# One of the last weight tiles of a decode step, shared out unevenly over the DMA engines

## The chip, the cores and the metric

The kernel runs on one core of a Trainium2 chip. The metric is the device time of one execution in microseconds (us). Everything is in float32.

## What is computed

One token goes through a layer norm and then through two parallel branches, sliding-window attention over a cache and a gated MLP; both are added to the token.

```
xn = layernorm(x)                                   # x: 1 x 1 x 1024
q  = xn @ wq                                        # 1024 x 4096, 32 heads of 128
k, v = the last 4096 positions of the cache         # 4 key/value heads, 8 query heads each
attn = softmax(q k^T / sqrt(128)) v @ wo            # wo: 4096 x 1024
mlp  = (gelu_tanh(xn @ w_gate) * (xn @ w_up)) @ w_down   # 1024 x 3584, 1024 x 3584, 3584 x 1024
y  = x + attn + mlp
```

With one token, every weight and cache row is used once: 94 MB are read.

## The kernel before, in words

All large tensors pass through one buffer in SBUF, `ring` (128 partitions, 176 KB each). `pieces` lists 20 pieces in the order in which they are loaded, each with its place in the ring and its size: wq in two pieces, keys, gate, values and up in two each, wo in two, and w_down in eight. `pump()` records the loads of all pieces whose place is free of pieces still in use; `done()` frees a piece when its last reader is recorded, and pumps again. All these loads are issued by SyncE (SP), in that order, on one DMA queue; three small loads of x go by ScalarE's queue. A load spans all 128 partitions.

w_down has 3584 rows; partition p holds 28 consecutive rows, and "tile t" is row t of every partition, a block of 128 partitions x 1024 columns (4 KB per partition, 512 KB in all). The pieces of w_down are tiles 0 to 11, 12 to 19, 20 and 21, 22 and 23, and then 24, 25, 26 and 27 alone; tile 27 comes in two halves of columns. So the loads get smaller toward the end.

TensorE and VectorE share the contractions. A tile on VectorE is one multiply-add into `part` (L213); a tile on TensorE is four or eight matmuls by `mm` (L158). The end of the program is written out by hand: tile 24 on TensorE into `sums`, then the product of `unit` with VectorE's partial sum `out_part` (a view of `part`), tile 25, an addition into `x_out` on VectorE, tile 26, and for each half of tile 27 its matmuls, one addition and two stores (one issued by SP, one by ScalarE).

The program is recorded first. `Program.add` notes what each operation reads and writes and derives what it must wait for; each DMA is a lane of its own with a semaphore of its own, and a reader waits until that semaphore has reached 16. `plan` drops waits that are already covered, `emit` writes the instructions.

Of the kernel before, what the change touches and what calls it, by code (L numbers as in the profile page):

```python
# [10 lines left out]
P = 128  # L11
# [13 lines left out]

RING = 176 * KB
SCRATCH = 1024
HEADS_A = [0, 2, 4, 6, 8, 10, 12, 14]
HEADS_B = [0, 2, 4, 6, 8, 10, 12, 14]
HID_A = [0, 2, 4, 6, 8]  # L30
# [5 lines left out]
class Program:  # L36

    def __init__(self, nc):  # L40
        self.nc = nc
        self.ops = []
        self.seen = {}
        self.engines = dict(pe=nc.tensor, dve=nc.vector, act=nc.scalar, pool=nc.gpsimd, sp=nc.sync)

    @staticmethod
# [5 lines left out]
        hi = lo + 1 + sum(abs(s) * (n - 1) for s, n in ap.ap[1:])  # L52
        return ap.tensor.name, p0, p0 + count, lo, hi

    def add(self, engine, emit, reads, writes, dma=False, tag=None):
        op = dict(engine=engine, emit=emit, dma=dma, needs={}, tag=tag, id=len(self.ops),
                  boxes=[self.box(a) for a in writes + reads])
        op["lane"] = f"dma{op['id']}" if dma else engine
        for writing, aps in ((False, reads), (True, writes)):
            for ap in aps:  # L60
                name, p0, p1, lo, hi = self.box(ap)
                for wrote, q0, q1, a, b, other in self.seen.get(name, ()):
                    if not (writing or wrote) or q0 >= p1 or p0 >= q1 or a >= hi or lo >= b:
                        continue
                    if other["lane"] == op["lane"] and (engine == "pe" or not wrote):
                        continue
                    lane = other["lane"]
                    op["needs"][lane] = max(op["needs"].get(lane, -1), other["id"])
        for writing, aps in ((False, reads), (True, writes)):
            for ap in aps:  # L70
                name, p0, p1, lo, hi = self.box(ap)
                kept = self.seen.setdefault(name, [])
                if writing:
                    kept[:] = [
                        k for k in kept
                        if not (p0 <= k[1] and k[2] <= p1 and lo <= k[3] and k[4] <= hi)
                    ]
                kept.append((writing, p0, p1, lo, hi, op))
        self.ops.append(op)
        return op  # L80

    def plan(self):
        known = {e: {} for e in self.engines}
        for op in self.ops:
            mine = known[op["engine"]]
            waits = []
            for lane, other in sorted(op["needs"].items(), key=lambda n: -n[1]):
                if mine.get(lane, -1) >= other:
                    continue
                waits.append(other)  # L90
                for k, v in self.ops[other]["after"].items():
                    mine[k] = max(mine.get(k, -1), v)
            op["waits"] = waits
            op["after"] = dict(mine)
            op["after"][op["lane"]] = op["id"]
        for op in self.ops:
            for other in op["waits"]:
                self.ops[other]["told"] = True
        counts = {}
        for op in self.ops:  # L100
            if op["dma"]:
                op["rank"] = 16
            elif op.get("told"):
                counts[op["engine"]] = counts.get(op["engine"], 0) + 1
                op["rank"] = counts[op["engine"]]
# [41 lines left out]
def decode_layer(nc, x, k_cache, v_cache, wq, wo, w_gate, w_up, w_down, out):  # L147
# [29 lines left out]
    def dve(call, reads, writes, engine="dve"):  # L177
        prog.add(engine, call, reads, writes)
# [9 lines left out]
    def add(o, a, b):  # L188
        dve(lambda e: e.tensor_add(o, a, b), [a, b], [o])  # L189
# [24 lines left out]
            [i, factor, other], [o],  # L214
        )

    def dma(engine, o, i, reads=(), writes=(), tag=None):
        return prog.add(
            engine, lambda e: e.dma_start(o, i), list(reads), list(writes), dma=True, tag=tag  # L219
        )  # L220

    ring = sbuf("ring", P, RING)
# [2 lines left out]
    def rows(w, a):  # L225
        return w[512 * a:512 * (a + 1), :].rearrange("(p r) n -> p (r n)", r=4)

    def heads_of(a):
        return wo[2048 * a:2048 * (a + 1), :].rearrange("(p t) n -> p (t n)", p=P)

    hidden_rows = w_down.rearrange("(p t) n -> p t n", p=P)
# [12 lines left out]
    def load(kind, i, at, size):  # L244
        slot = ring[:, at * KB:(at + size) * KB]
        held[kind, i] = slot
        if kind == "v":
            src = v_cache[0, 2 * i:2 * i + 2, SK - WIN:, :].rearrange("g (p j) d -> p g (j d)", p=P)
            dma("sp", slot.rearrange("p (g n) -> p g n", g=2), src, writes=[slot], tag=(kind, i))
        elif kind == "k":  # L250
            src = k_cache[0, 2 * i:2 * i + 2, SK - WIN:, :].rearrange("g (s j) d -> s g (j d)", g=2, j=64)
            dma("sp", slot, src, writes=[slot], tag=(kind, i))
        elif kind == "d":
            lo, hi = i
            halves = 2 if lo == TD - 1 else 1
            wide = slot.rearrange("p (t n) -> p t n", n=D)
            for half in range(halves):
                cols = slice(half * D // halves, (half + 1) * D // halves)
                dst = wide[:, :, cols]
                dma("sp", dst, hidden_rows[:, lo:hi, cols], writes=[dst], tag=(kind, i, half))  # L260
        else:
            src = {
                "q": lambda: rows(wq, i), "g": lambda: rows(w_gate, i), "u": lambda: rows(w_up, i),
                "o": lambda: heads_of(i),
            }[kind]()
            dma("sp", slot, src, writes=[slot], tag=(kind, i))
# [4 lines left out]
    def pump():  # L271
        while queue:
            kind, i, at, size = queue[0]
            if any(at < hi and lo < at + size for lo, hi in live.values()):
                return
            load(*queue.pop(0))
            live[kind, i] = (at, at + size)
# [170 lines left out]
    p = rows_sb[:, 0, :]  # L448
# [159 lines left out]
    def head(t):  # L608
        return oz[:, 32 * t:32 * t + 64]
# [38 lines left out]
    def contract(kind, i, z, dve_tiles, rows):  # L648
        w = held[kind, i].rearrange("p (t n) -> p t n", n=D)
        count = w.shape[1]  # L650
        rest = [(z(t), w[:, t, :]) for t in range(count) if t not in dve_tiles]
        if rows:
            tiles_on_rows(rest)
        else:
            for pair in rest:
                tile_on_pe(*pair)
        for t in dve_tiles:
            tile_on_dve(z(t), w[:, t, :])
        done(kind, i)
# [38 lines left out]

    state["total"] = 2 * TO + 12 - len(HEADS_A + HEADS_B + HID_A)
    contract("o", 0, head, HEADS_A, True)  # L700
    contract("o", 1, lambda t: head(TO + t), HEADS_B, True)
    contract("d", (0, 12), column, HID_A, True)
    add(out_part, acc[:].rearrange("p a n -> p (a n)"), out_part)
    contract("d", (12, 20), lambda t: column(12 + t), HID_B, False)
    contract("d", (20, 22), lambda t: column(20 + t), HID_C, False)
    contract("d", (22, 24), lambda t: column(22 + t), HID_D, False)
    tile_on_pe(column(24), held["d", (24, 25)])
    tile_on_pe(unit[:], out_part)
    tile_on_pe(column(25), held["d", (25, 26)], True)
    add(x_out[:].rearrange("p f n -> p (f n)"), sums[:], x_out[:].rearrange("p f n -> p (f n)"))  # L710
    for half in range(2):
        half_on_pe(column(26), held["d", (26, 27)], half, True, False)
    stores = out.rearrange("a b (f c n) -> (a b) f c n", f=2, c=4)
    for half in range(2):
        half_on_pe(column(27), held["d", (27, 28)], half, False, True)
        add(y[:, half, :], acc[:, half, :P], x_out[:, half, :])
        for k, engine in enumerate(("sp", "act")):
            src = y[31 + 64 * k:33 + 64 * k, half, :]
            dma(
                engine, stores[0, half, 2 * k:2 * k + 2, :], src, reads=[src],  # L720
                tag=("out", half, k),
            )
# [25 lines left out]
```

## Time and profile before

| | us |
|---|---|
| median of 3 runs | 226.66 |
| lowest and highest | 226.65, 226.82 |
| profiled execution | 226.83 |
| its span in the profile | 225.5 |

| engine | share of the span busy |
|---|---|
| VectorE (DVE) | 64% |
| TensorE (PE) | 39% |
| ScalarE (ACT) | 12% |
| the 16 DMA engines, SP's queue (q1) | 97.5% |

A row of the profile names the line of the kernel, the engine, the operation, and what is written from what (`ring<-in_B_w_down` is a load of w_down into the ring, `SPq` the queue of SP that issues it). "us to landing" is the time from a load's issue until its data is there. DMA is the mean busy share of the 16 DMA engines. A wait stands in brackets behind a row, with what ended it.

### The profile page before, as it was taken

How to read it: one execution, taken by the hardware profiler on the slowest of the kernel's cores; microseconds unless marked ns; L12 is line 12 of the kernel's file. 1: busy time of each engine (PE TensorE's matmuls, PEld its weight loads, DVE VectorE, ACT ScalarE, POOL GpSimd, SP SyncE). 2: the span in 40 equal slices, each digit the busy share in tenths (PEclk: the TensorE clock that was granted, in tenths of full speed). 3: DMA queues.
4: the chain of work that ended last, by engine and by line, in shares of the span. 5: the costliest groups of instructions: out<-in, count | busy, mean ns of one | idle time of the engine just before them, and what ended most of it. 6: DMA issues, size and time to landing. Idle time of an engine off the chain costs nothing.

```text
span 225.5 us, 1396 instructions
## 1 busy us (share of the span) xinstructions
PE 87.5 (39%) x574; PEld 34.8 (15%) x574; DVE 143.2 (64%) x127; ACT 26.3 (12%) x45; POOL 0.7 (0%) x6
## 2 busy tenths in 40 slices
PE   1200000007699007989002537137339204408475
PEld 0100000006263002462000111011002001002131
DVE  7500998499727990000998699869538804938691
ACT  2000000004555001482000300200000000000000
POOL 1000000000000000000000000000000000000000
PEclk9999999999999755999755667857855855965889
DMA  9899899899989999999999998999999999999992
GB/s 373 372 395 535 372 395 535 349 405 478 468 349 426 465 401 503 427 397 471 427 397 392 433 509 387 478 391 491 419 395 488 419 395 413 427 439 442 382 405 111
DMA packets 3317, 94.46 MB, mean 419 GB/s; under 512 B 350, under 2 KB 366, under 8 KB 1008
## 3 DMA queue, kind: packets, MB, share of 16 engines
q1 hardware_dynamic: 3288, 94.38, 97.5%
q8 instruction: 4, 0.07, 0.1%
q10 hardware_dynamic: 24, 0.01, 0.0%
q14 instruction: 1, 0.01, 0.0%
HBM read 94.38 MB, written 0.00 MB: 419 GB/s over the span
## 4 chain that ended last, share of the span: by engine, by line
DMA 65%; DVE 26%; PE 7%; issue 1%; SPq 1%; DVEq 0%
DVE part L213 24%; DMA ring<-in_B_w_down 19%; DMA ring<-in_A_wq 18%; DMA ring<-in_B_w_gate 15%; DMA ring<-in_A_wo 13%; PE acc L158 3%; PE tp L163 2%; PE s_p L158 2%; DVE part L209 1%; SPq L219 1%; DVE rows_sb L186 0%; DVE part L189 0%; DVEq L118 0%; SPq L118 0%
## 5 line engine op out<-in xcount | busy, mean ns | idle before, releaser
L213 DVE SCALAR_TENSOR_TENSOR part<-ring,xz,part 128x3584 f32<-128x3584 f32 (+1 forms) x19 | 78.8, 4148 | 26.6 <-DMA ring<-in_B_w_gate 22.6
L163 PE MATMUL tp<-ident,ring 128*128 128x128 f32 x128 | 20.3, 303 | 44.4 <-DMA ring<-in_A_k_cache 42.8
L213 DVE SCALAR_TENSOR_TENSOR part<-ring,oz,part 128x1024 f32<-128x1024 f32 x15 | 19.3, 1285 | 9.9 <-DMA ring<-in_A_wo 9.4
L172 ACT ACTIVATE ring<-tp 128x512 f32<-128x512 f32 x32 | 18.1, 596 | 58.4 <-PE tp L163 58.0
L163 PEld LDWEIGHTS tp<-ident,ring 128*128 128x128 f32 x128 | 15.0, 152 | 51.2 <-DMA ring<-in_A_k_cache 42.9
L209 DVE TENSOR_SCALAR part<-ring,xz 128x3584 f32<-128x3584 f32 (+1 forms) x3 | 6.5, 2176 | 19.7 <-DMA ring<-in_A_wq 12.1
L158 PE MATMUL acc<-ring,oz 128*32 128x512 f32 x64 | 11.7, 899 | 16.8 <-DMA ring<-in_A_wo 16.8
L213 DVE SCALAR_TENSOR_TENSOR part<-ring,hz,part 128x1024 f32<-128x1024 f32 x10 | 12.8, 1285 | 6.1 <-DMA ring<-in_B_w_down 5.8
L158 PE MATMUL acc<-part,unit 128*32 128x448 f32 (+1 forms) x48 | 7.3, 742 | 22.3 <-DVE part L213 22.3
L158 PE MATMUL o_p<-ring,pT 128*32 128x512 f32 x64 | 11.0, 847 | 7.1 <-DMA ring<-in_A_v_cache 6.5
L158 PE MATMUL acc<-ring,hz 128*32 128x128 f32 (+1 forms) x60 | 8.0, 616 | 10.1 <-DMA ring<-in_B_w_down 10.1
L158 PE MATMUL s_p<-ring,qz 128*32 128x512 f32 x64 | 9.3, 598 | 0.0
L163 PE MATMUL tp<-ident,rows_sb 128*128 128x128 f32 x16 | 3.5, 361 | 12.0 <-ACT rows_sb L172 11.8
L158 PE MATMUL sums<-ring,hz 128*32 128x256 f32 x72 | 6.2, 482 | 4.7 <-DMA ring<-in_B_w_down 4.7
L158 PEld LDWEIGHTS acc<-ring,oz 128*32 128x32 f32 x64 | 2.5, 155 | 26.6 <-DMA ring<-in_A_wo 19.4
L158 PEld LDWEIGHTS acc<-part,unit 128*32 128x32 f32 x48 | 1.4, 126 | 26.4 <-DVE part L213 24.2
L172 ACT ACTIVATE rows_sb<-s_p,negm 128x512 f32<-128x512 f32 x2 | 1.4, 687 | 30.4 <-DVE negm L209 30.4
L158 PEld LDWEIGHTS o_p<-ring,pT 128*32 128x32 f32 x64 | 2.6, 149 | 14.5 <-issue 13.4
L158 PE MATMUL acc<-ring,xz 128*32 128x448 f32 x32 | 4.8, 767 | 0.0
L158 PEld LDWEIGHTS acc<-ring,hz 128*32 128x32 f32 x60 | 2.2, 135 | 15.8 <-issue 14.0
L163 PEld LDWEIGHTS tp<-ident,rows_sb 128*128 128x128 f32 x16 | 2.3, 179 | 15.5 <-ACT rows_sb L172 13.6
L158 PEld LDWEIGHTS sums<-ring,hz 128*32 128x32 f32 x72 | 2.4, 136 | 9.2 <-DMA ring<-in_B_w_down 7.3
(85 smaller groups left out, 47.8 us busy)
## 6 DMA issues: line engine op xcount, KB each, us to landing
ring<-in_B_w_gate SPq DMA_DIRECT2D x2, 7168.0 KB, 31.9
ring<-in_B_w_up SPq DMA_DIRECT2D x2, 7168.0 KB, 33.9
ring<-in_A_k_cache SPq DMA_DIRECT2D x2, 4096.0 KB, 39.7
ring<-in_A_v_cache SPq DMA_DIRECT2D x2, 4096.0 KB, 34.8
ring<-in_B_w_down SPq DMA_DIRECT2D x1, 6144.0 KB, 42.9
ring<-in_B_w_down SPq DMA_DIRECT2D x1, 4096.0 KB, 38.8
ring<-in_B_w_down SPq DMA_DIRECT2D x2, 1024.0 KB, 40.4
ring<-in_B_w_down SPq DMA_DIRECT2D x3, 512.0 KB, 42.0
```

Of the source, the lines that this page charges most:

```text
L158: "pe", lambda e: e.matmul(o, lhsT, rhs, start=start, stop=stop),
L163: prog.add("pe", lambda e: e.transpose(o, i, eye), [i, eye], [o])
L172: "act", lambda e: e.activation(o, i, func, scale=scale, **kw),
L209: dve(lambda e: e.tensor_scalar(o, i, s1, s2, op0=op0, **kw), reads, [o])
L213: lambda e: e.scalar_tensor_tensor(o, i, factor, other, op0=ALU.mult, op1=ALU.add),
L219: engine, lambda e: e.dma_start(o, i), list(reads), list(writes), dma=True, tag=tag
```

## The change

Tile 24 of w_down no longer comes as one transfer of 128 partitions but as ten. Each takes every second, fourth or eighth partition of some stretch, and together they take each of the 128 once: 64, 26, 13, 5, 5, 4, 2, 3, 3 and 3 partitions. All ten share one semaphore, and the reader waits until it has reached 160. All other pieces stay as they are.

```diff
+UNEVEN = 24
+SHARES = [
+    (0, 128, 2), (1, 102, 4), (3, 100, 8), (7, 40, 8), (47, 80, 8), (87, 112, 8), (119, 128, 8),
+    (105, 114, 4), (117, 126, 4), (107, 124, 8),
+]
...
-    def add(self, engine, emit, reads, writes, dma=False, tag=None):
+    def add(self, engine, emit, reads, writes, dma=False, tag=None, group=None):
...
-        op["lane"] = f"dma{op['id']}" if dma else engine
+        op["lane"] = engine
+        if dma:
+            first = self.groups.setdefault(group, op["id"]) if group else op["id"]
+            op["lane"] = f"dma{first}"
+            self.sizes[op["lane"]] = self.sizes.get(op["lane"], 0) + 16
...
-                    if other["lane"] == op["lane"] and (engine == "pe" or not wrote):
+                    if other["lane"] == op["lane"] and (engine == "pe" or dma or not wrote):
...
-                op["rank"] = 16
+                op["rank"] = self.sizes[op["lane"]]
...
             lo, hi = i
+            if lo == UNEVEN:
...
+                for share in SHARES:
+                    some = slice(*share)
+                    dma(
+                        "sp", slot[some, :], hidden_rows[some, lo, :], writes=[slot],
+                        tag=(kind, i), group=(kind, i),
+                    )
+                return
```

A triple in `SHARES` is first partition, end and step. On SP the loads of the pieces of w_down stand before the change in this order (partitions x elements of a partition; the three of 128x1024 are tiles 24, 25 and 26, the two of 128x512 the halves of tile 27):

```order
L219 DMA ring<-in_A_wo 128x16384 x2
L219 DMA ring<-in_B_w_down 128x12288
L219 DMA ring<-in_B_w_down 128x8192
L219 DMA ring<-in_B_w_down 128x2048 x2
L219 DMA ring<-in_B_w_down 128x1024 x3
L219 DMA ring<-in_B_w_down 128x512 x2
L219 DMA out_y<-part 2x128 x2
```

The first of the three is what the change replaces; the same stretch of SP after it (the same helper stands at L230 now):

```order
L230 DMA ring<-in_B_w_down 128x2048 x2
L230 DMA ring<-in_B_w_down 64x1024
L230 DMA ring<-in_B_w_down 26x1024
L230 DMA ring<-in_B_w_down 13x1024
L230 DMA ring<-in_B_w_down 5x1024 x2
L230 DMA ring<-in_B_w_down 4x1024
L230 DMA ring<-in_B_w_down 2x1024
L230 DMA ring<-in_B_w_down 3x1024 x3
L230 DMA ring<-in_B_w_down 128x1024 x2
L230 DMA ring<-in_B_w_down 128x512 x2
L230 DMA out_y<-part 2x128 x2
```

Nine issues more stand ahead of tiles 25, 26 and 27; the instructions of the other engines are the same in the same order.

More of the change, by code (lines that the diff above doesn't have):

```diff
@@ L43, in __init__ @@
         self.seen = {}
+        self.groups, self.sizes = {}, {}
         self.engines = dict(pe=nc.tensor, dve=nc.vector, act=nc.scalar, pool=nc.gpsimd, sp=nc.sync)
@@ L215, in multiply_add, with dma @@
         )
-    def dma(engine, o, i, reads=(), writes=(), tag=None):
+    def dma(engine, o, i, reads=(), writes=(), tag=None, group=None):
         return prog.add(
-            engine, lambda e: e.dma_start(o, i), list(reads), list(writes), dma=True, tag=tag
+            engine, lambda e: e.dma_start(o, i), list(reads), list(writes), dma=True, tag=tag,
+            group=group,
         )
@@ L254, in load @@
             lo, hi = i
+            if lo == UNEVEN:
+                assert sorted(p for s in SHARES for p in range(*s)) == list(range(P))
+                for share in SHARES:
[5 more added lines that the diff above has]
+                return
             halves = 2 if lo == TD - 1 else 1
```

## The prediction

> **What bounds the kernel now.** I read the page's DMA part first, then the end of the chain of waits, then the transfers and TensorE in the last microseconds.
>
> ```profile
> span 225.5 us, 1396 instructions
> DMA packets 3317, 94.46 MB, mean 419 GB/s; under 512 B 350, under 2 KB 366, under 8 KB 1008
> q1 hardware_dynamic: 3288, 94.38, 97.5%
> q8 instruction: 4, 0.07, 0.1%
> ```
>
> The 16 DMA engines are busy 97.5% of the span with the loads that SP issues: the kernel is a stream of weights. The question is only when the last byte of that stream arrives. The chain of waits ends so (start, length, what):
>
> ```profile
> 180.03 0.43 SPq L219
> 180.46 0.04 issue
> 180.50 42.73 DMA ring<-in_B_w_down
> ...
> 223.28 0.47 PE acc L158 x8
> 223.75 0.02 issue
> 223.77 0.29 DVE part L189
> ```
>
> The last half of tile 27 is the end of the chain; behind it stand four matmuls with their weight loads (0.47 us), one addition (0.29 us) and the stores, which the change leaves alone. So a last byte that comes x earlier ends the kernel x earlier, unless TensorE becomes late (below). How the stream ends is seen in the transfers from 220 to 224 us, in slices of 0.1 us (first row: busy tenths of the 16 engines; second: GB/s):
>
> ```profile
> DMA  9799998995645433322322112100000000000000
> GB/s 389 266 512 389 369 389 307 451 348 184 225 164 225 164 143 143 123 102 102 143 102 82 61 41 82 41 21 20 0 0 0 0 0 0 0 0 0 0 0 0
> ```
>
> This is the important row. To 220.9 us nearly all engines work; then the rate falls, and the last byte comes at 222.8. One engine carries 434/16 = 27.1 GB/s when all run (the mean GB/s of the stretch 45 to 100 us):
>
> ```profile
> 45.00:100.00 55.00, 31.73 (x204) 17.34 (x204) 31.34 (x19) 18.76 (x33) 0.00 (x0) 0.88 1.01 434
> ```
>
> So 143 GB/s at 221.5 is about five engines, 102 at 222.0 about four, some 60 (mean of the next three) two, and 20 at 222.7 one. I read the finishing times as 222.8, 222.65, 222.3 and 222.2 for the four latest, about 221.9 for a fifth, and 220.9 to 221.5 for the other eleven. They all move the same bytes, so five fell behind earlier. From 220.9 on the row sums to 2168 GB/s x 0.1 us = 217 KB; at 434 GB/s that is 0.50 us, so a perfect division would end at 221.4: no division of the rows can gain more than 1.4 us.
>
> One cause shows in the instruction queue (q8, page above: four packets, 0.07 MB, so 16 KB each). In the stretch 215 to 226 us:
>
> ```profile
> q8 instruction: 1, 0.02, 0.6%
> ```
>
> 0.6% of 16 engines x 11 us is 1.06 us of one engine for one fetch of 16 KB, which the engine's own rows wait out. Four fetches, each on one engine, would make four engines late by a microsecond or more, about what the tail shows. The rows do not name the engines. Following single packets through the trace, which no view prints, I find the four fetches on four different engines, and the two engines that carry the two-partition loads of x among the early ones.
>
> **The change, part by part.** Tile 24 is 128 rows of 4 KB, today eight on each engine. Ten transfers take its place. I take equal shares on the largest number of engines up to 16 that divides the partitions, counted from engine 0; the title's thirteen engines for 26 and 13 fit that. The 350 packets under 512 B bear out the division in a small case: 21 loads of 128 partitions leave 21 x 16 = 336 completion writes, and seven transfers of two partitions (three loads of x, four stores) leave 14 if each runs on two engines; 336 + 14 = 350. Then 64 rows give four to every engine, 26 and 13 give three more to engines 0 to 12, and 5, 5, 4, 2, 3, 3, 3 go to the lowest. Rows of tile 24: engines 0 and 1 fourteen, 2 thirteen, 3 ten, 4 nine, 5 to 12 seven, 13 to 15 four. [...]
>
> The price of a row comes from TensorE, which waits for each of the last tiles:
>
> ```profile
> start us, us, engine line op out<-in xcount [idle before <-releaser]
> 219.49 0.64 PE L158 MATMUL sums<-ring,hz 128*32 128x256 f32 x8 [0.62 <-DMA ring<-in_B_w_down]
> 219.94 0.62 PE L158 MATMUL sums<-part,unit 128*32 128x256 f32 x8
> 220.78 0.64 PE L158 MATMUL sums<-ring,hz 128*32 128x256 f32 x8 [0.21 <-DMA ring<-in_B_w_down]
> 222.03 1.04 PE L158 MATMUL acc<-ring,hz 128*32 128x128 f32 x24 [0.61 <-DMA ring<-in_B_w_down]
> 223.28 0.43 PE L158 MATMUL acc<-ring,hz 128*32 128x128 f32 x8 [0.21 <-DMA ring<-in_B_w_down]
> ```
>
> Tiles 24, 25 and 26 start at 219.49, 220.78 and 222.03: 1.27 us for eight rows, 0.157 us a row. So 13 to 15 finish 4 x 0.157 = 0.63 us earlier, 5 to 12 0.16 earlier, 4 is 0.16 later, 3 0.31, 2 0.79, 0 and 1 0.94.
>
> Which of them are late decides the sum. If the two latest and one of the next two are 13 to 15, their ends become 222.2, 222.0 and 221.7; the fourth, among 5 to 12, goes from 222.3 to 222.15; engines 0 to 2, if early (up to 221.2), come to 222.0 to 222.15. All meet near 222.2: 0.6 us less. If the latest stands among 5 to 12, 0.16 less; if it is 0 or 1, 0.94 more. Between these ends I take 0.6: the two engines that can be told, 0 and 1, are early and have 1.3 us of room for 0.94, and of the fourteen others, among which the four latest must be, nothing in the rows speaks against 13 to 15.
>
> Nine more completion writes on the lowest engines are bounded by 0 and by what the stream leaves idle: 2.5% (q1 at 97.5%) of the 1.27 us of a tile, 0.03 us for nine packets. I take 0.03.
>
> SP's issues:
>
> ```profile
> L219 SPq DMA_DIRECT2D ring<-in_B_w_down x9: 328/328/10887, 160.6 to 180.5; - x9
> 180.50 10.89 SPq L219 DMA_DIRECT2D ring<-in_B_w_down  x1
> ring<-in_B_w_down SPq DMA_DIRECT2D x3, 512.0 KB, 42.0
> 189.05 10.53 DVE L213 SCALAR_TENSOR_TENSOR part<-ring,oz,part 128x1024 f32<-128x1024 f32 x8 [9.43 <-DMA ring<-in_A_wo]
> 203.59 6.57 DVE L213 SCALAR_TENSOR_TENSOR part<-ring,hz,part 128x1024 f32<-128x1024 f32 x5 [4.00 <-DMA ring<-in_B_w_down]
> 213.30 6.57 DVE L213 SCALAR_TENSOR_TENSOR part<-ring,hz,part 128x1024 f32<-128x1024 f32 x5 [1.82 <-DMA ring<-in_B_w_down]
> ```
>
> Nine more at 0.33 us are 3.0 us of SP (3.9 at 0.43, the dearest unblocked step in the chain). Tiles 25, 26 and 27 are queued behind them. The cover is the distance from issue to landing, 42.0 us for tiles 24 to 26, so I cost them at nothing. One row warns: the very last issue took 10.89 us, to 191.4. Something was full. If it is full by packets per engine, engines 0 and 1 get fifteen more (six rows, nine completions). The tiles ahead pass nine packets of an engine each (eight rows and a completion), in 203.59 - 189.05 = 14.5 us and 213.30 - 203.59 = 9.7 us, so fifteen take 14.5 + 6/9 x 9.7 = 21 us: the last issue would go at about 212, still 8 us before its rows are due. The first share carries the slot's old wait, the others none, and no other engine waits for SP before the stores.
>
> What is late next: tile 24 at 218.9 and tile 25 at 220.2 find TensorE held by the product with out_part, which waits for VectorE:
>
> ```profile
> 219.92 0.16 PEld L158 LDWEIGHTS sums<-part,unit 128*32 128x32 f32 x8 [0.28 <-DVE part L213]
> ```
>
> It ends at 219.94 + 0.62 = 220.56, tile 25 at 221.2, and tile 26 comes at 221.4: TensorE stays ahead by 0.2 us, so all of the gain arrives.
>
> Sum: 226.83 (this profiled execution: span 225.5 and 1.33 around it) - 0.60 + 0.03 = 226.26. The median of the runs is 226.66, 0.17 lower; from it the forecast is **226.1**.
>
> **Rivals.** *Ports instead of engines (nothing, or a loss).* Perhaps the 27.1 GB/s belongs to the place written rather than to the engine. Then a late engine's partitions still have to take the same bytes, and handing its rows to others relieves nothing: while it writes its earlier rows, up to eight rows of tile 24 come into its partitions from elsewhere (up to 8 x 0.157 = 1.26 us), for which it saves eight rows and spends four (0.63) on foreign ones. Net between 0.2 less, where foreign rows fall into gaps, and 0.63 more; 226.5 to 227.3, middle 226.8. [...]
>
> *A late engine among 2 to 4 (slower).* If one of the four that end at 222.2 to 222.8 is engine 2, it ends 0.79 later, as engine 3 or 4 0.31 or 0.16: the kernel takes up to 0.79 us more, 226.7 to 227.45. It decides once engine 2 ends after 222.0 today (222.8 - 0.79). Against it: three of fourteen engines, and four late ones to place; for it: nothing names them.
>
> *The late ones are not 13 to 15, or the shares fall otherwise.* The latest among 5 to 12 gives 226.5; shares that spread over all 16 engines give 226.7. Two completion packets for two partitions speak against the latter.
>
> *The queue is full by transfers, not packets (slower).* If the 10.89 us came from nine transfers outstanding, the ten of tile 24 fill it alone: tile 25 could be issued only when the first shares have landed, near 218.5, and the engines run empty. The last store
>
> ```profile
> L219 SPq DMA_DIRECT2D out_y<-part x2: 257/294/331, 223.5 to 224.1; - x2
> ```
>
> is issued at 224.1 and the span ends at 225.5, so a transfer on empty engines takes over 1 us; one to three such gaps give 227.7 to 229.7. Against it: the oldest of the nine, the second half of wo, had landed by 189.05 (it releases VectorE there), and the issue went on only at 191.4, when packets of the next tile had passed.
>
> **How the numbers follow.** Relief of 13 to 15 as summed: 0.40, own range 225.9 to 226.2. Ports: 0.33, of which 0.25 within 0.2% and 0.08 slower. Not 13 to 15, or spread otherwise: 0.10, the same. Engine 2, 3 or 4 late: 0.10. Full queue: 0.07. A measurement of this kernel can tell about 0.2% (0.45 us) from no change. Faster 0.40; same 0.25 + 0.10 = 0.35; slower 0.08 + 0.10 + 0.07 = 0.25. Low is 225.9, the first case with 0.2 us to spare; high is 227.3, the end of the ports case, which leaves out the queue and a late engine 2.
>
> **What would show it.** In the slices from 220 us the fall should start later and be steeper, with the last byte near 222.2; the matmuls of tile 27's second half near 222.7. Packets under 512 B should be 350 - 16 + 16 + 13 + 13 + 5 + 5 + 4 + 2 + 3 + 3 + 3 = 401. If ports set the pace, the slices before 220.9 show lower rates than before and the last byte stays at 222.8 or later. A late low engine shows as one engine (20 to 27 GB/s) alone for up to a microsecond. A full queue shows as zeros in the slices. Wrong would be my numbering of engines or the guess that fetches hit the high ones.

## The result, and the profile after

The changed kernel takes 227.38 us (median of 8 runs, 227.13 to 227.74) against 226.75 for the kernel before (8 runs, 226.53 to 226.90): ratio 1.0028, 95% interval 1.0017 to 1.0039. It is 0.63 us slower, and outside the range that was given. The profiled execution is the slowest of the eight, 227.74 us. Its page:

```profile
span 226.4 us, 1405 instructions
DMA packets 3368, 94.46 MB, mean 417 GB/s; under 512 B 401, under 2 KB 417, under 8 KB 1059
q1 hardware_dynamic: 3339, 94.38, 97.6%
```

The bytes are the same, the engines are as busy as before (97.6% against 97.5%), and the 401 small packets are what the division of the shares called for. What changed is the rate. The transfers from 220 to 224 us after the change, in slices of 0.1 us (busy tenths of the 16 engines, GB/s), to be laid beside the row that the prediction started from:

```profile
DMA  9959999989899999866464456453432101000000
GB/s 369 492 225 430 410 369 451 430 348 451 328 410 430 348 389 471 307 225 225 184 246 184 184 205 246 164 205 123 184 123 82 41 21 41 0 0 0 0 0 0
```

The fall starts later, as forecast (221.6 instead of 220.9), but it isn't steeper: 184 to 246 GB/s is seven to nine engines at 27.1, and the last byte comes at 223.4 instead of 222.8. Half of the engines are late now, where five were: of the sixteen landings of the last transfer, eight come by 222.45 us and eight from 223.19 on; before, eleven came by 221.98 and five from 222.35 on. They fell behind earlier. From 214 to 224 us in slices of 0.25 us, first the kernel before:

```profile
DMA  9998979899998999999999999997543321000000
GB/s 393 459 459 360 492 328 426 361 410 426 393 475 328 410 426 360 426 377 410 442 377 434 361 426 377 393 410 262 213 156 123 123 90 57 33 0 0 0 0 0
```

and the kernel after:

```profile
DMA  9999798997999999999998999999999555431000
GB/s 459 426 393 492 328 459 361 377 475 311 492 328 279 279 311 229 262 262 262 262 295 262 344 344 377 393 410 410 369 393 369 197 197 229 180 139 57 16 0 0
```

The two agree to 217.0 us. Then the rate after drops to 229 to 311 GB/s, comes back to 344 at 219.5 and to 410 at 220.5; in these three microseconds tile 24 comes (its single landings, read from the trace, run from 216.9 to 220.3). All the while the first row shows 9: no engine is idle, each packet only takes longer. Single packets, which no view prints, say the same: those of 4 KB that start between 217.0 and 219.5 us take 0.23 to 0.25 us (medians of half microseconds, nine in ten over 0.21) where they took 0.16 before. As one stretch (DMA share and GB/s are the last two columns), before and after:

```profile
217.00:220.00 3.00, 1.67 (x32) 0.43 (x28) 2.80 (x3) 0.00 (x0) 0.00 (x0) 1.00 1.00 398
```

```profile
217.00:220.00 3.00, 1.29 (x16) 0.16 (x8) 2.54 (x3) 0.00 (x0) 0.00 (x0) 0.88 1.02 283
```

398 - 283 = 115 GB/s over 3 us are 345 KB that did not arrive; at 434 GB/s they take 0.8 us. That is about what was lost: the last byte is 0.6 us later, its landing 0.72. TensorE passes it on:

```profile
218.91 0.64 PE L169 MATMUL sums<-ring,hz 128*32 128x256 f32 x8 [1.26 <-DMA ring<-in_B_w_down]
220.35 0.64 PE L169 MATMUL sums<-ring,hz 128*32 128x256 f32 x8 [0.81 <-DMA ring<-in_B_w_down]
220.81 0.76 PE L169 MATMUL sums<-part,unit 128*32 128x256 f32 x8
221.46 1.08 PE L169 MATMUL sums<-ring,hz 128*32 128x256 f32 x8
222.71 1.94 PE L169 MATMUL acc<-ring,hz 128*32 128x128 f32 x32 [0.18 <-DMA ring<-in_B_w_down]
```

The first row belongs to the piece with tiles 22 and 23, the second is tile 24: 220.35, where it was 219.49. The chain ends

```profile
186.00 36.67 DMA ring<-in_B_w_down
222.67 0.04 issue
222.71 1.98 PE acc L169 x32
224.71 0.29 DVE part L200
```

Here the last transfer in the chain is tile 26, and all matmuls of tiles 26 and 27 follow in one row of 32. That belongs to this execution: TensorE's granted clock is 0.50 from 222.5 to 223.5 us (1.00 before), and 32 matmuls took 1.98 us.

```profile
222.50:223.50 1.00, 0.82 (x20) 0.74 (x20) 0.42 (x1) 0.00 (x0) 0.00 (x0) 0.50 0.26 98
```

The last landing moved from 223.23 to 223.95 us (single landings, read from the trace; no view prints them), and TensorE's clock adds about 0.2: together the 0.91 us by which this execution, 227.74, is over the profiled one of before, 226.83. In k1_one_52 below TensorE has full clock there, and the late end is left: the last landing at 223.98, the profiled execution 227.57 us.

### The profile page after: what moved, and what is told of

Its sections match the earlier page's. It is cut to its first block, busy times and chain, and to the rows that moved or that the text cites. A ratio compares the mean times of both kernels' runs of the same rounds, so it can differ in the third digit from the quotient of the medians.

```text
span 226.4 us, 1405 instructions
## 1 busy us (share of the span) xinstructions
PE 91.3 (40%) x574; PEld 36.3 (16%) x574; DVE 143.3 (63%) x127; ACT 25.9 (11%) x45; POOL 0.7 (0%) x6
## 3 DMA queue, kind: packets, MB, share of 16 engines
q1 hardware_dynamic: 3339, 94.38, 97.6%
## 4 chain that ended last, share of the span: by engine, by line
DMA 70%; DVE 17%; PE 7%; SPq 3%; ACT 1%; issue 1%; DVEq 0%
DMA ring<-in_A_v_cache 18%; DMA ring<-in_B_w_down 16%; DVE part L224 15%; DMA ring<-in_B_w_gate 13%; DMA ring<-in_A_wo 13%; DMA ring<-in_A_wq 10%; PE o_p L169 6%; SPq L230 3%; DVE part L220 2%; PE acc L169 1%; PE tp L174 1%; ACT rows_sb L183 0%; DVE m L212 0%; ACT pT L183 0%; DVE part L200 0%
## 5 line engine op out<-in xcount | busy, mean ns | idle before, releaser
L224 DVE SCALAR_TENSOR_TENSOR part<-ring,xz,part 128x3584 f32<-128x3584 f32 (+1 forms) x19 | 78.8, 4148 | 27.1 <-DMA ring<-in_B_w_gate 23.1
L183 ACT ACTIVATE ring<-tp 128x512 f32<-128x512 f32 x32 | 17.8, 596 | 60.8 <-PE tp L174 60.8
L220 DVE TENSOR_SCALAR part<-ring,xz 128x3584 f32<-128x3584 f32 (+1 forms) x3 | 6.5, 2175 | 17.8 <-DMA ring<-in_A_wq 11.9
L169 PE MATMUL acc<-part,unit 128*32 128x448 f32 (+1 forms) x48 | 9.4, 931 | 20.4 <-DVE part L224 20.4
L169 PE MATMUL o_p<-ring,pT 128*32 128x512 f32 x64 | 12.7, 968 | 7.8 <-DMA ring<-in_A_v_cache 7.1
L169 PE MATMUL acc<-ring,hz 128*32 128x128 f32 (+1 forms) x60 | 7.5, 638 | 8.8 <-DMA ring<-in_B_w_down 8.8
L169 PE MATMUL sums<-ring,hz 128*32 128x256 f32 x72 | 6.8, 513 | 6.1 <-DMA ring<-in_B_w_down 6.1
L169 PEld LDWEIGHTS acc<-part,unit 128*32 128x32 f32 x48 | 1.7, 148 | 25.6 <-DVE part L224 22.5
L169 PE MATMUL acc<-ring,xz 128*32 128x448 f32 x32 | 5.7, 881 | 0.0
L169 PEld LDWEIGHTS sums<-ring,hz 128*32 128x32 f32 x72 | 2.2, 131 | 10.8 <-DMA ring<-in_B_w_down 9.7
## 6 DMA issues: line engine op xcount, KB each, us to landing
ring<-in_B_w_down SPq DMA_DIRECT2D x2, 512.0 KB, 36.3
```

Source lines behind the costliest of these rows:

```text
L169: "pe", lambda e: e.matmul(o, lhsT, rhs, start=start, stop=stop),
L183: "act", lambda e: e.activation(o, i, func, scale=scale, **kw),
L220: dve(lambda e: e.tensor_scalar(o, i, s1, s2, op0=op0, **kw), reads, [o])
L224: lambda e: e.scalar_tensor_tensor(o, i, factor, other, op0=ALU.mult, op1=ALU.add),
```

## The experiments

Three explanations stood: **meeting**, that an engine loses where another engine writes the same place of SBUF at the same time (the prediction's rival *Ports instead of engines*); **counts**, that uneven shares or more rows on the low engines cost the time; and **the ten transfers themselves**, their issues and completions. The expectations speak of theories of *ports*, of *imbalance* and of *transfers*; there *small ports* are places of eight partitions, and *halves* is the guess that each half of the partitions has one limit and nothing finer matters. Which partitions share a place, and which rows of a transfer an engine takes, is assumed in them; no profile prints either. The kernel before took 226.69 to 226.71 us (medians) in all these comparisons. A triple is first partition, end, step, as in the diff.

### Which partitions share a place: rows of 64 KB

To see single packets, five kernels leave tile 24 whole and cut the first half of wq (64 KB for each partition), whose rows take 2.42 us each at full rate. The edit, with the shares that follow:

```diff
+            if (kind, i) == ("q", 0):
...
+                for share in SHARES:
+                    some = slice(*share)
+                    dma("sp", slot[some, :], src[some, :], writes=[slot], tag=(kind, i), group=(kind, i))
+                return
```

**w1_wq_halves**: (0, 64, 1), (64, 128, 1).

> Tile 24 in one transfer again. The first load of the stream, half of wq (128 partitions x 64 KB, 19.4 us at 27.1 GB/s an engine), comes as partitions 0-63 and 64-127. Every engine still gets eight rows of 64 KB. Ports theory (eight partitions share one way in of 27.1 GB/s, and an engine has one for itself only when a transfer is cut so that it writes its own eight): in each half two engines write at one place, so the half goes at about 217 GB/s: 38.7 us instead of 19.4, the kernel about 19 us longer. Imbalance theory (tile 24's loss comes from fourteen rows on the lowest engines) and transfers theory (it comes from many small transfers and their completions): no change, within 0.5 us.

248.28 us, 21.6 more. All engines work, at half the rate:

```profile
10.00:15.00 5.00, 0.00 (x0) 0.00 (x0) 0.72 (x5) 0.00 (x0) 0.00 (x0) 1.00 1.02 210
```

A packet takes 5.12 us, not 2.42. So 27.1 GB/s is not the engine's limit alone: which partitions are loaded at one time counts too.

**w2_wq_middle**: (32, 96, 1), (0, 32, 1), (96, 128, 1).

> As the last one, but cut as partitions 32-95, 0-31 and 96-127. Again eight rows of 64 KB on every engine. Ports theory: 32-95 in blocks of four gives each engine its own place, so these 4 MB go at 434 GB/s (9.7 us); the two quarters put two engines at one place, 217 GB/s, 9.7 us each: 29 us instead of 19.4, the kernel about 10 us longer, and the rate in the stretch shows first full, then half. Imbalance and transfers theories: no change, within 0.5 us.

237.53 us, 10.8 more. The same number of neighbouring partitions, from 32 on, runs at full rate, and the two outer quarters at half:

```profile
5.00:10.00 5.00, 1.18 (x4) 1.01 (x4) 3.10 (x19) 0.20 (x1) 0.00 (x0) 1.00 1.00 433
...
15.00:20.00 5.00, 0.00 (x0) 0.00 (x0) 0.00 (x0) 0.00 (x0) 0.00 (x0) 1.00 1.02 210
```

**w3_wq_even_odd**: (0, 128, 2), (1, 128, 2).

> As the last two, cut as even and odd partitions, the step of tile 24's largest share. Ports theory: with four rows in a block on each engine, engines four apart write at one place, half rate, the kernel about 19 us longer; if they drift apart in phase, less. Imbalance and transfers theories: no change, within 0.5 us.

227.34 us in one run, all packets but the first of each engine 2.42 us, as before: a miss for the half rate expected, for which the 64 rows had been cut into sixteen stretches of neighbours. The time is 0.63 us over the kernel before, more than the other theories allowed; 0.3 us of it is there at the start (the first large packet starts at 2.07 instead of 1.78 us), and for the rest one run shows no cause. The kernel's first transfer is of this kind, the 64 even partitions, so that one is innocent.

**x1_wq_blocks**: the nine stretches (0, 8), (8, 24), (24, 40), ... (104, 120), (120, 128), step 1.

> Tile 24 whole again; the first half of wq in blocks of 16 neighbouring partitions (8-23, 24-39, ... 104-119, with 0-7 and 120-127 alone), one 64 KB row on each of the 16 engines a block. Two theories are left after the cut of wq in halves doubled its time and the cut in even and odd did not. Small ports: eight partitions share 27.1 GB/s, a block of 16 neighbours reaches four such places, 109 GB/s, 9.7 us a block: the load takes about 72 us, the kernel about 53 us longer. Halves: partitions 0-63 and 64-127 share 217 GB/s each and nothing finer matters: 4.8 us a block, but 2.4 us for the block 56-71 that lies in both halves: about 36 us, the kernel about 17 us longer.

295.26 us, 68.6 more; a packet of the sixteen-row transfers takes 9.38 us, four times 2.42 within 3%:

```profile
15.00:50.00 35.00, 0.00 (x0) 0.00 (x0) 0.00 (x0) 0.00 (x0) 0.00 (x0) 1.00 1.08 120
```

**x2_wq_step8**: every eighth partition, eight transfers.

> [...] Small ports: engines four apart write at one place, the load takes 39 us instead of 19, the kernel about 19 us longer. Halves: eight engines in each half, full rate, the kernel within 0.8 us of before.

248.07 us, 21.4 more, packets of 5.1 us: half rate (210 GB/s from 10 to 30 us). Together: 0 to 63 run at 210 GB/s, 32 to 95 at 433, sixteen neighbours at 120, every eighth partition at 210. And 32 to 63 add nothing to 0 to 31, which alone (a quarter in w2_wq_middle) run at 210 too. The rates that the theory of *ports* gave for these cuts (217, 434, 109 and half of 434) come within about a tenth; the half rate that it gave for the even and the odd partitions fails. That eight partitions share a place is my estimate, which these rates allow; which eight, they leave open. Which engine writes which rows no run shows.

One rival is left beside this. Each partition has its own stretch of the source, so these cuts change the places read together with the places written. Neighbouring rows are 64 KB apart in wq and 112 KB in w_down, and neighbours lose in both (here, and in t3_contig below), which speaks for the partitions; but no run changes one without the other.

### The change undone in part

**t1_even_odd**: tile 24 as (0, 128, 2), (1, 128, 2): two transfers, eight rows on each engine.

> Tile 24 in two transfers, even and odd partitions: four rows each on every engine, eight in all, as before. Small ports theory: the same cut of wq ran at full rate, so no engine meets another: the time of before within 0.25 us. Transfers theory (each further transfer costs by itself): 0.05 to 0.1 us more. Imbalance theory: no change.

226.76 us (11 runs), ratio 1.0004, 0.9995 to 1.0012: no difference. Its rate does not drop from 217 us on: 396 GB/s to 220 us, packets of 4 KB at 0.16 us (slices as above, from 214 us):

```profile
DMA  8989999889998899999999899997423221000000
GB/s 360 492 360 393 492 393 426 328 344 524 377 459 344 344 442 344 475 377 410 442 360 467 311 434 385 393 426 279 172 107 131 98 90 66 16 0 0 0 0 0
```

**c1_step8**: tile 24 as eight transfers of every eighth partition, again eight rows on each engine.

> [...] Small ports theory: the tile's 1.27 us becomes up to 2.7, and neighbours in phase are slowed: 0.5 to 1.4 us slower than before, with no unevenness in the counts at all. Imbalance theory: no change. Transfers theory: 0.1 to 0.3 us slower.

229.19 us, ratio 1.011 (1.0096 to 1.0123): 2.5 us slower with perfectly even counts. That is more than I expected from half rate over one tile (1.27 us at full); the direction is clear, the size is open. Its packets of 4 KB take 0.21 to 0.35 us from 216 to 221 us (medians of half microseconds), at times over twice 0.16, and over far more than 1.27 us.

```profile
DMA  9997999799899999996999999989989899986432
GB/s 492 492 393 295 426 492 442 295 344 311 213 279 197 295 197 180 229 164 164 311 295 246 262 262 230 262 262 295 410 320 418 344 442 361 401 336 238 172 123 106
```

**t3_contig**: the ten counts of the change (64, 26, 13, 5, 5, 4, 2, 3, 3, 3) on neighbouring partitions.

> The changed kernel's ten counts (64, 26, 13, 5, 5, 4, 2, 3, 3, 3) on neighbouring partitions instead of spread ones. Small ports theory: the transfer of 64 now meets itself (partitions 0 to 63 reach eight places), and the small ones lie on one or two places: slower than the changed kernel by 0.3 to 1.5 us, 227.7 to 228.9. Imbalance theory: the same as the changed kernel, 227.1 to 227.7.

229.39 us, ratio 1.0115 (1.0099 to 1.013). The counts on each engine are those of the change, the time is 2.0 us longer than with its steps of 2, 4 and 8: which partitions come at one time decides, and the spreading in the change avoids most of the loss, not all. It lost more than the 227.7 to 228.9 of the expectation. Packets of 4 KB take 0.27 to 0.43 us from 216 to 221 us, and the stretch that had 398 GB/s before and 283 with the change has

```profile
217.00:220.00 3.00, 1.53 (x16) 0.40 (x8) 1.44 (x2) 0.00 (x0) 0.00 (x0) 0.69 1.00 183
```

**t5_ten_sems**: each of the ten transfers with a semaphore of its own (`group` left out).

> The changed kernel with a semaphore of its own for each of the ten transfers, so that TensorE waits ten times and the landings of each transfer can be told apart. All theories: the time of the changed kernel within 0.4 us (227.0 to 227.8). The transfers of 26 and 13 partitions should show thirteen landings each; if engines 13 to 15 are the late ones, the three largest delays that the landings of 64 partitions show are missing there.

247.44 us, and no answer: without the group each of the ten waited until the one ahead had landed, since the program notes the whole slot as written by each. By the chain such a step takes 2.0 to 2.7 us:

```profile
230.34 2.02 DMA ring<-in_B_w_down
232.38 2.16 DMA ring<-in_B_w_down
234.56 2.08 DMA ring<-in_B_w_down
```

**t5_ten_sems_b**: the same without these waits.

> The changed kernel with ten semaphores, this time without the waits of each transfer for the one before (which my first version had by mistake, and which made it 20 us longer). All theories: 227.0 to 227.8. The landings of 26 and 13 partitions, thirteen each, should lack the three latest engines if those are 13 to 15.

227.28 us in one run, like the change: no cost of the shared semaphore is seen.

### Which engines are late, and whether they can be relieved

**i1_find_late**: (0, 128, 2), then odd partitions in shares of 15, 14, 12, 10, 8 and 5, each with its own semaphore.

> Which engines are late: tile 24 in transfers of 64, 15, 14, 12, 10, 8 and 5 partitions, each with a semaphore of its own, so that an engine's number shows in which transfers it takes part. From the ten semaphores of the changed kernel I read that of the five late engines one is number 3 (the mildest), two of the three latest stand among 13 to 15, and two more among 5 to 12. So the transfers of 15 and 14 partitions should miss one or two of the three latest, that of 12 two, and that of 5 show one late landing. Time: 226.7 to 228, not what it is for.

227.64 us in one run. If a share of n rows uses the lowest n engines, as the prediction assumed (the rows of the changed kernel fit it, below; the numbers are names that no row prints), the number of landings that come a microsecond after the others tells who is late. Of 64 rows on 16 engines five landings are late (218.5 to 219.6 us, the others by 217.4), of 15 also five, of 14 four, of 12, 10 and 8 three each, of 5 one. So 14 is late, one of 12 and 13, two of 5 to 7, one of 0 to 4, and 15 isn't. In t5_ten_sems_b the shares of 26 and of 13 rows (13 engines) have three late landings each, so 12 isn't late and 13 is; the share of 4 has a late landing and those of 3 have none, so the low one is engine 3. Matched by nearest landing, 13 is the latest and 14 the second (the expectations of k1_one_52 and k2_four_low below had put the second among 5 to 7). Four late engines beside the mildly late 3 fit the four fetches of q8 (four packets on the pages of before and after); which engine a fetch was on is not shown.

**r1_same_half**: (0, 128, 2), (1, 102, 4), (3, 104, 4), (105, 128, 2): by the prediction's division nine rows on engines 0 to 11, eight on 12, four on 13 to 15.

> [...] Halves theory: little is lost to the crowded half, the relief of 13 to 15 (0.6 us) mostly arrives: 0.2 to 0.5 us faster than before, 226.2 to 226.5. Small ports theory: engines four apart still meet in the transfer of 64 and in those of 26: slower than before by 0.3 us or more. Imbalance theory (fourteen rows on the lowest were the fault, not the places): 0.4 to 0.6 us faster.

227.57 us (5 runs), ratio 1.004 (1.0026 to 1.0054): slower with four transfers instead of ten, and no engine above nine rows. Of the three theories only small ports had said slower; the stretch from 217 to 220 us has 284 GB/s, about as with the change (283).

**k1_one_52**: the same rows per engine, but the 52 odd ones up to 103 in one transfer: (0, 128, 2), (1, 104, 2), (105, 128, 2).

> Tile 24 in three transfers: 64 even partitions, the 52 odd ones from 1 to 103 in one (thirteen engines, four neighbouring odd rows each), the last 12 odd ones. Rows per engine are the same as in r1_same_half (nine on engines 0 to 11, eight on 12, four on 13 to 15); only the cutting of the 52 differs: there two transfers of 26, each with a step of four. Theory of counts (uneven shares or more rows on the low engines cost the time): as r1_same_half, 227.5 to 227.7. Theory of meeting (an engine loses where another writes the same place of SBUF in the same moment): 116 of the 128 rows go where nobody else writes, twelve meet an engine, so most of the loss goes: 226.7 to 227.1. Theory of relief as in the prediction, with the late engines as the landings of i1_find_late place them (the latest is 13, the next among 5 to 7): 13 is relieved by 0.63, the next gets one row more, 222.65 + 0.16 = 222.8, nothing gained: 226.7.

227.63 us, ratio 1.0046 (1.0033 to 1.006). The forecast of my theory (226.7 to 227.1) failed, and that of counts came out. Its rate drops as that of the change does, which pointed to the geometry rather than to the theory: I had taken eight neighbours for one place.

```profile
DMA  9999999699989897979999999999999863221000
GB/s 459 393 393 426 426 459 410 262 459 442 410 213 360 197 262 197 311 229 377 360 262 295 377 328 369 434 369 361 434 369 377 303 229 123 115 90 57 25 0 0
```

**y1_wq_52**: the cut of k1_one_52, on the first half of wq, tile 24 whole.

> Tile 24 whole; the first half of wq (64 KB for each partition) in the three transfers of k1_one_52: 64 even partitions, the 52 odd ones up to 103, the last 12 odd ones. k1_one_52 missed what I expected, because I took eight neighbouring partitions for one place. [...] Theory of meeting: ten of the packets of 64 KB take about 5.1 us and three 2.42 through four rows, 4 x 2.7 = 10.8 us more for the engines that meet, and up to 5 for the last twelve rows, which two by two enter places whose own engine is at work: 237 to 243. Theory of counts (only the nine, eight and four rows matter): one row more, 2.42: 229 to 230, all packets 2.42.

244.55 us, 17.8 more where counts alone allowed 2.4 (a little above the 237 to 243 of meeting). The 64 even rows run at full rate, the 52 at half, on all engines (the DMA share stays at 1.0), so also on those that have no row of the 52 and have gone on to their next transfer:

```profile
5.00:10.00 5.00, 1.17 (x4) 1.00 (x4) 3.10 (x19) 0.20 (x1) 0.00 (x0) 1.00 1.00 433
10.00:15.00 5.00, 0.00 (x0) 0.00 (x0) 0.72 (x5) 0.00 (x0) 0.00 (x0) 1.00 1.38 407
15.00:20.00 5.00, 0.00 (x0) 0.00 (x0) 0.00 (x0) 0.00 (x0) 0.00 (x0) 1.00 1.02 210
```

Packets 2.42 us through the first transfer, 5.1 through the second. Which engines meet and which do not was my estimate; the packets show no such split. So the cut of k1_one_52 crowds, and the theory of counts, which allowed no slower packet, falls.

**k2_four_low**: as k1_one_52, the last twelve rows as (105, 124, 6), (107, 126, 6), (109, 128, 6), so on engines 0 to 3, and none more on the late ones among 5 to 7.

> As k1_one_52, but the last 12 odd rows come as three transfers of four, so on engines 0 to 3, three rows more for each: eleven rows on 0 to 3, eight on 4 to 12, four on 13 to 15. Theory of counts: 227.5 or more, since engines 0 to 3 have eleven. Theory of meeting: twelve rows in others' places as in k1_one_52, on four engines: 226.7 to 227.1. Theory of relief: 13 and 14 relieved by 0.63, the engine among 5 to 7 that ends at 222.65 untouched and now the latest: 0.15 less, 226.55. If meeting and relief both hold, 226.6 to 227.0.

227.48 us, ratio 1.004 (1.0026 to 1.0054). The 226.7 to 227.1 of meeting and the 226.55 of relief failed here too. It crowds as k1_one_52 does (284 GB/s from 217 to 220 us), so whether relief is left once the crowding is away was not seen. Whether an uneven division can be had without crowding no run shows: r1_same_half, k1_one_52 and this one have 284, 296 and 284 GB/s in that stretch. No version that was run beats the kernel before; t1_even_odd ties with it.

## Why the prediction was wrong, by its steps

- **What bounds the kernel**: right. The loads set the end before and after, the engines are busy 97.6% of the span, and of the 0.91 us between the two profiled executions 0.72 is the last landing.
- **Rows per engine and small packets**: the 401 came out to the packet: the semaphore of tile 24 has 67 landings, 16 + 13 + 13 + 5 + 5 + 4 + 2 + 3 + 3 + 3, and nine events more at the issues of the nine shares on fewer than sixteen engines (single events of the profiled execution, read from the trace). In t5_ten_sems_b, too, each share has as many landings as the division gives it engines (and, where these are fewer than sixteen, one event more at its issue). The rows came out as well: joined end to start, the single packets of the profiled execution form, in the best fit found, sixteen chains with 14, 14, 13, 10, 9, eight times 7 and three times 4 rows of tile 24. That is an estimate from packet times: how many rows each share has was given to the fit, which chains take the small shares was not. In it they fall on the same few engines. The numbers 0 to 15 are names for this order, on which the reading of i1_find_late rests; no row prints them (the title, which the prediction called on for the thirteen, does not name them).
- **The price of a row: the step that failed.** 0.157 us (1.27/8 is in fact 0.159, and so long most single 4 KB packets take before) is right for whole transfers, and for the even and the odd partitions of t1_even_odd (0.16 us a packet). The step carried it over to rows handed to other engines, and kept it for the rows of the engines that were to be relieved. The evidence was only of whole transfers. In the change a packet of 4 KB took 0.23 to 0.25 us while tile 24 passed (nine in ten over 0.21, so nearly all engines were slowed), and the mean rate was 283 instead of 398 GB/s: 345 KB less in 3 us, 0.8 us of the stream, against a relief of 0.60. That the slowing comes from engines that meet at a place of SBUF is inferred from the cuts: t3_contig, with the same counts, has 183 GB/s, and t1_even_odd 396. In w1_wq_halves, where all rows crowd, a packet takes 2.1 times as long (5.12 instead of 2.42 us).
- **Which engines are late**: nearly right, and a guess: the prediction had only that nothing spoke against 13 to 15. By i1_find_late 13 and 14 are the two latest and the next two are among 5 to 7; by the prediction's own terms this still gives about 222.2, so a wrong choice of engines does not account for the loss. The late engines were slowed before their own saving came: the landings of the piece ahead, tiles 22 and 23, end on the four slowest engines at 217.3, 217.7, 218.0 and 218.2 us before and at 217.5, 218.4, 218.8 and 218.9 after, when the early engines were already at tile 24 (its first rows landed at 216.9).
- **Nine more completions** at 0.03 us: not seen apart. t1_even_odd has sixteen more (two transfers instead of one) and shows 0.07 us, within its interval.
- **SP's issues cost nothing**: right, though their price was not. The nine more took 0.61 to 0.94 us each (single issues, read from the trace), not 0.33 to 0.43. The 18 issues of the pieces of w_down and their waits end at 160.36 + 48.48 = 208.84 us (the prediction said about 212), and tiles 25 and 26, queued behind, still have 36.3 us from issue to landing.

```profile
160.36 48.48 SPq L230 DMA_DIRECT2D ring<-in_B_w_down  x18
...
ring<-in_B_w_down SPq DMA_DIRECT2D x2, 512.0 KB, 36.3
```

- **TensorE stays ahead by 0.2 us**: could not show, since no gain arrived; at granted clock 0.50 it even fell behind tile 26 in the profiled execution.
- **Rival ports instead of engines** (0.33): what happened, as far as the cuts can tell the place written from the place read. Its two signs, lower rates in the slices ahead of the fall and a last byte no earlier than 222.8, are both there. Its upper end of 0.63 more is what was measured, but by luck: it counted four foreign rows at 0.157 us on one late engine, and what happened is a lower rate on nearly all engines for 3 us. 227.3, the high end of the range, was counted from the lower median of the three runs shown. Of its 0.33 only 0.08 stood for slower.
- **Rivals of a late low engine and of other late engines**: engine 3 is late, but mildly, and no engine is alone at the end (eight are late together). **Full queue**: no zeros in the slices before the end.

## What to carry to other kernels

Before rows are moved from one DMA engine to another, ask what the rate of an engine belongs to: if the place written has the same limit, a row handed over costs more than its price on a free engine (1.5 times in the change, twice where all rows crowd), and it can slow the engine it was to relieve (here the four slowest landed tiles 22 and 23 by 218.9 us, where it was 218.2). A transfer of the whole 128 partitions, or of every second one, ran at full rate here; other cuts must be judged by the places that they reach at one time, not by rows per engine. In the profile the sign is a DMA row full of 9s over a falling GB/s row.

## What the runs showed of the hardware that I had not expected

- 64 partitions are not equal to 64 partitions: 0 to 63 ran at 210 GB/s, 32 to 95 and the even ones at 433.
- If two engines share each place in w1_wq_halves (an estimate from its half rate), they move a little less together than one alone: 2 x 64 KB in 5.12 us are 25.6 GB/s, one alone 27.1. In x1_wq_blocks 9.38 us a packet are 27.9 GB/s for four, by the same reckoning, so the loss does not grow with their number.
- One transfer that crowds slows engines that have gone on to other transfers: in y1_wq_52 thirteen engines had the 52 crowded rows (350 - 16 + 16 + 13 + 12 = 375 packets under 512 B, which its page has), and all sixteen ran at half rate (210 GB/s from 15 to 20 us, DMA share 1.02).
